# One block's forward and backward pass: weight-gradient products dealt out in pieces

## The chip, the cores and the metric

The kernel runs on one core of a Trainium2 chip. The metric is device time in microseconds of one execution, lower is better. The kernel before took 1703.19 us (median of three runs, 1692.96 to 1707.07). Profiles are of one execution each, with instructions per engine, waits and DMA transfers. TensorE (PE) multiplies matrices, VectorE (DVE) and ScalarE (ACT) do elementwise work, GpSimd (POOL) issues some DMAs and gathers, SyncE (SP) issues most DMAs.

## The reference

A transformer-like block with modulation (adaLN) is run forward, and then all its gradients are taken. x is 2048 tokens by 1024 features, the MLP is 1024 to 3584 to 1024, everything is bf16.

```python
def _A_ref(x, w_r, w_i):              # spectral mixer
    X = rfft2(x.astype(float32))
    return irfft2(X * (w_r + 1j * w_i), s=(S, D)).astype(bfloat16)

def _B_ref(x, w1, b1, w2, b2):        # MLP
    y = _layernorm(x)
    h = _gelu(einsum('bsd,df->bsf', y, w1) + b1)
    return einsum('bsf,fd->bsd', h, w2) + b2

mod = (_silu(c) @ w_mod).reshape(1, 6, 1, -1)
sa, ca, ga, sb, cb, gb = (mod[:, r] for r in range(6))
x = A_x
h = _layernorm(x) * (1 + ca) + sa
x = x + ga * _A_ref(h, A_w_r, A_w_i)
h = _layernorm(x) * (1 + cb) + sb
x = x + gb * _B_ref(h, B_w1, B_b1, B_w2, B_b2)
out, vjp = jax.vjp(f, A_x, A_w_r, A_w_i, B_w1, B_b1, B_w2, B_b2, c, w_mod)
return (out, *vjp(grad_out))
```

Outputs are out_0 (the block's result) and out_1 to out_9: gradients of x, of the spectral weights (out_2, out_3), of w1 (out_4), b1, w2 (out_6), b2, c (out_8) and w_mod (out_9).

## The kernel before, in words

Tokens are handled in four blocks of 512 (4 tiles of 128). The Fourier transforms are matrix products with cosine and sine matrices, with even and odd halves folded. The stages in code order, with the times they take in the profile:

- *Start and forward spectral mixer* (0 to some 305 us). `spectral_core` makes the forward product over tokens (`s_fwd`, matmuls "pu"), eight `pair` steps (matmuls "pcs" over features, then DVE work that multiplies with w_r and w_i and writes rows of R), the inverse over tokens (`s_inv`, matmuls "pv", four classes CE, SE, CO, SO of 32 matmuls), and four output steps (matmuls "po", then `consume`, a long DVE and ACT chain). The products "pp" (L610, gradient through w2) run beside it.
- *MLP* (389 to 864). `z_block(b, g0, g1)` makes groups g0 to g1 of the seven hidden groups of block b: 32 matmuls "pz", then gelu and its derivative on ACT and DVE; h goes to an SBUF slot (eleven in a ring) and to DRAM (d_hh), the gradient to DRAM (d_gz). `bo_pass(b, h)` makes half h of the output product: seven pieces of 16 matmuls "pbo", one per hidden group, into four PSUM banks; then eviction, the product with grad_out, its column sum "pa" on PE, and the store of out_0. The order is `z_block(b, 0, 4)`, `bo_pass(b-1, 1)`, `z_block(b, 4, 7)`, `bo_pass(b, 0)`.
- *Backward through w1 and layer norm* (864 to 1142): matmuls "pg", then DVE and ACT work per block, which ends in fbuf2, the input of the backward spectral pass.
- *Backward spectral pass and w2 gradient* (1078 to 1457). The second `spectral_core`, with `consume_bwd` as its output step; behind it in code order the w2 gradient: 28 chunks of 128 hidden rows, each one transposed load of d_hh and two products of 16 matmuls "gw2acc" with gB (grad_out times the gb row).
- *w1 gradient* (1457 to 1701): seven blocks of 512 hidden columns, each two transposed loads of d_gz (gzh) and eight products of 16 matmuls "gw1acc". Between them the gradient of w_mod: six rows r of 1024 values (d_gmod, fp32), broadcast to all partitions and cast; per row eight loads of w_mod, eight outer-product tiles stored to out_9 (gww) and eight reductions (wrw).

PSUM has tags "s" and "d" with two banks each and "f" with four; gw2acc, gw1acc, pbo, pp and pg use "f". SBUF tiles share buffers by tag: a tile of one tag must be free before the next one of that tag is written.

The order of the instructions in each engine's queue is fixed when the kernel is built: a planner takes the operations with code order as their priority and with estimated times, so that later code may be drawn forward where an engine would stand idle by the estimate. `tc.high_priority()` moves an operation ahead; `nc.any` leaves it to the planner whether ACT or DVE does it. Waits on the chip are by semaphore, and an engine does not pass the instruction at the head of its queue.

Of the kernel before, what the change touches and what calls it, by code (L numbers as in the profile page):

```python
# [10 lines left out]
FP32 = mybir.dt.float32  # L11
# [6 lines left out]
P = 128  # L18
# [12 lines left out]
NB = 4  # L31
# [4 lines left out]
def kernel(  # L36
# [74 lines left out]
    d_gmod = dram.tile([6 * D], FP32, name="d_gmod")  # L111
# [58 lines left out]
    def store_gmod(accs, r):  # L170
        for h in range(2):
            row = small.tile([1, KH], FP32, tag="gmrow", bufs=1)
            nc.vector.tensor_copy(out=row[:], in_=accs[h][0:1, :])
            nc.sync.dma_start(out=d_gmod[r * D + h * KH:r * D + (h + 1) * KH].rearrange("(o n) -> o n", o=1), in_=row[:])
# [234 lines left out]
    def spectral_core(fwd, fb, sms, em, css, pt, evac_u, evac_c, evac_v, consume, o4tag, pfs=None):  # L409
# [83 lines left out]

        for cl in (CE, SE, CO, SO):
            Us[cl] = s_fwd(cl, fb, sms[cl % 2][:, cl // 2], evac_u)
# [14 lines left out]
        for par in range(2):  # L510
            for m in range(4):
                pair(par * 4 + m, par, m)
        for cl in (CE, SE, CO, SO):
            s_inv(cl, smis[cl % 2])
        ct = reg.tile([P, 4, 4, D], BF16, name="ct", tag=o4tag)
        xts = [reg.tile([P, 4, D], BF16, name="xt", tag=tg)[:] for tg in ("sma", "smb")]
        for i in range(4):
            o4 = ct[:, 3 * (i % 2)]
            for cl in range(4):
                for hh_ in range(2):  # L520
                    po = ps_d("po")
                    for d2 in range(2):
                        dc = 2 * hh_ + d2
                        for h in range(2):
                            gi = 2 * dc + h + (4 if (dc >= 2 and cl >= 2) else 0)
                            nc.tensor.matmul(po[:, d2 * 256:(d2 + 1) * 256], lhsT=Vs[cl][:, 2 * dc + h, i * P:(i + 1) * P],  # L526
                                             rhs=gm[:, gi, :], start=(h == 0), stop=(h == 1))
                    with tc.high_priority():
                        nc.any.tensor_copy(out=o4[:, cl, hh_ * 512:(hh_ + 1) * 512], in_=po[:])
            consume(i, o4, ct[:, 1 + i % 2], xts[i % 2])  # L530

# [156 lines left out]
    def bo_pass(b, h):  # L688
# [4 lines left out]
        for g in range(7):  # L693
            wp = w2p[w2n[0] % 4]
            w2n[0] += 1
            nc.sync.dma_start(out=wp, in_=w2_v[:, g * 4:(g + 1) * 4, cs_])
            hh = hh_slots[(b * 7 + g) % 11]
            for i in range(4):
                for k in range(4):
                    nc.tensor.matmul(pbs[i][:], lhsT=hh[:, k, i * P:(i + 1) * P], rhs=wp[:, k, :],  # L700
                                     start=False, stop=(g == 6 and k == 3))
        bo, x1t, go = (otile[:, k] for k in range(3))
# [5 lines left out]
        tt(go, go, bo, ALU.mult)  # L708
        pa = ps_d("pa")
# [6 lines left out]
        tt(bo, bo, bcn(gb_row[:, cs_], 4), ALU.mult)  # L716
        tt(bo, bo, x1t, ALU.add)
        store_tok_half(out_0, bo, b, h)
# [9 lines left out]
    nc.sync.dma_start(out=d_gmod[5 * D:6 * D].rearrange("(o n) -> o n", o=1), in_=gacc)  # L728
# [81 lines left out]
    store_gmod(accS, 3)  # L810
    store_gmod(accC, 4)
# [21 lines left out]
    hh_o = [0, 1, 0, 1] + [2, 3, 0, 1] * 6  # L833
# [4 lines left out]
    def consume_bwd(i, o4, tmp, n1):  # L838
# [21 lines left out]
        if i == 3:  # L860
            store_gmod(accCA, 1)

    spectral_core(False, fbuf2, (smA2, smB2), em2, [css2[:, 0], css2[:, 1]],
                  new_pair_temps(["t0", "t1", "t2", "t3"]), act_copy, act_copy, act_copy, consume_bwd, "fr", pfs)


    gwo = reg.tile([P, 2, D], BF16, name="gwo", tag="ph")
# [5 lines left out]
    for fc in range(NFC):  # L873
        nc.sync.dma_start_transpose(out=hh_s[hh_o[fc]], in_=d_hh[fc * P:(fc + 1) * P, :])
        if fc >= NFC - 2:
            continue
        ob = gwo[:, fc % 2]
        for h in range(2):
            acc = ps_f("gw2acc")
            for t in range(NT):  # L880
                gw2_mm(acc, fc, h, t)
            with tc.high_priority():
                nc.scalar.copy(out=ob[:, h * KH:(h + 1) * KH], in_=acc[:])  # L883
        nc.gpsimd.dma_start(out=out_6[fc * P:(fc + 1) * P, :], in_=ob)
    last = [(fc, h, ps_f("gw2acc")) for fc in (NFC - 2, NFC - 1) for h in range(2)]
    for b in range(NB):
        for fc, h, acc in last:
            for t in range(4 * b, 4 * b + 4):
                gw2_mm(acc, fc, h, t)
    for fc, h, acc in last:  # L890
        with tc.high_priority():
            nc.scalar.copy(out=gwo[:, fc % 2, h * KH:(h + 1) * KH], in_=acc[:])
        if h == 1:
            nc.gpsimd.dma_start(out=out_6[fc * P:(fc + 1) * P, :], in_=gwo[:, fc % 2])

    n3ns = []
    for b in range(NB):
        n3n = reg.tile([P, 4, D], BF16, name=f"n3n{b}", tag=f"t{b}")
        nc.sync.dma_start(out=n3n[:], in_=chunk_rows(d_n3, b))
        n3ns.append(n3n)  # L900
    gzh = [reg.tile([P, 8, 512], BF16, name=f"gzh{k}", tag=PXT[2 + k]) for k in range(4)]
    gwo1 = reg.tile([P, 4, 512], BF16, name="gwo1", tag="ph")

    def gw1_load(fg):
        for k in range(2):
            ins = nc.sync.dma_start_transpose(out=gzh[2 * (fg % 2) + k][:], in_=d_gz[fg * 512:(fg + 1) * 512, k * 1024:(k + 1) * 1024])  # L906
        return ins

    def gw1_block(fg):
        gz2 = gzh[2 * (fg % 2):2 * (fg % 2) + 2]  # L910
        for cch in range(NDC):
            acc = ps_f("gw1acc")
            for t in range(NT):
                nc.tensor.matmul(acc[:], lhsT=n3ns[t // 4][:, t % 4, cch * P:(cch + 1) * P], rhs=gz2[t // 8][:, t % 8, :],  # L914
                                 start=(t == 0), stop=(t == NT - 1))
            ob = gwo1[:, (fg * NDC + cch) % 4]
            with tc.high_priority():
                nc.scalar.copy(out=ob, in_=acc[:])  # L918
            nc.gpsimd.dma_start(out=out_4[cch * P:(cch + 1) * P, fg * 512:(fg + 1) * 512], in_=ob)  # L919

    gw1_load(0)
    gw1_block(0)
# [3 lines left out]
    for b in range(NB):  # L926
# [7 lines left out]
    store_gmod(accGA, 2)  # L934
# [6 lines left out]
    nc.sync.dma_start(out=d_gmod[0:D].rearrange("(o n) -> o n", o=1), in_=sr[0:1, 0, 0, :])  # L941

    u_bfc = small.tile([P, NDC], BF16, tag="u_bfc", bufs=1)
    nc.vector.tensor_copy(out=u_bfc[:], in_=u_col[:])
    u_rt = small.tile([P, NDC], FP32, tag="u_rt", bufs=1)
    nc.vector.tensor_copy(out=u_rt[:], in_=u_bfc[:])
    gr = [reg.tile([P, 2, D], FP32, name=f"gr{k}", tag=f"uv{k}") for k in range(2)]
    wrw = reg.tile([P, 4, D], BF16, name="wrw", tag="uv2")
    gww = reg.tile([P, 4, D], BF16, name="gww", tag="uv3")
    nn = 0  # L950
    for ri, r in enumerate((5, 3, 4, 1, 2, 0)):
        with tc.issue_after(gw1_load(1 + ri).ins):
            grep_ = gr[ri % 2][:, 0, :]
            gbf = gr[ri % 2][:, 1, 0:KH].bitcast(BF16)
            nc.sync.dma_start(out=grep_, in_=d_gmod[r * D:(r + 1) * D].partition_broadcast(P))
            nc.vector.tensor_copy(out=gbf, in_=grep_)
            for jc in range(NDC):
                wr = wrw[:, nn % 4, :]
                gw = gww[:, nn % 4, :]
                nn += 1  # L960
                nc.sync.dma_start(out=wr, in_=w_mod[jc * P:(jc + 1) * P, r * D:(r + 1) * D])
                nc.vector.tensor_scalar(out=gw, in0=gbf, scalar1=u_rt[:, jc:jc + 1], scalar2=None, op0=ALU.mult)
                nc.gpsimd.dma_start(out=out_9[jc * P:(jc + 1) * P, r * D:(r + 1) * D], in_=gw)  # L963
                nc.vector.tensor_tensor_reduce(out=wr, in0=wr, in1=gbf, scale=1.0, scalar=0.0,
                                               op0=ALU.mult, op1=ALU.add, accum_out=gu[:, r, jc:jc + 1])
        gw1_block(1 + ri)
# [41 lines left out]
```

## Time and profile before

| | before |
|---|---|
| time, median of three runs | 1703.19 us |
| the profiled execution's own time | 1712.4 us |
| its span | 1710.6 us |
| PE busy | 1493.2 us (87%) |
| DVE busy | 1066.1 us (62%) |
| ACT busy | 742.0 us (43%) |
| POOL busy | 370.8 us (22%) |
| mean granted TensorE clock | 0.949 |

How to read it: the slices cut the span into 40 equal parts of 42.8 us and give each engine's busy share in tenths. A matmul's busy time overlaps with the next one's, so counts per stretch say more than busy time. A wait is written as engine, what it was about to do, and who ended the wait. A group of instructions is given with its count, busy time, mean length in ns and the idle time before it. In the DMA list stand the count, the size of one and the median time from issue to landing.

### The profile page before, as it was taken

To read this page: it belongs to the slowest core of one execution; us is meant where nothing else is said; L and a number is where in the kernel's file an instruction comes from. 1 tells how busy PE (TensorE), PEld (TensorE's weight loads), DVE (VectorE), ACT (ScalarE), POOL (GpSimd) and SP (SyncE) were. 2 spreads that over 40 slices of the span, in tenths; PEclk is the share of its full clock that TensorE was granted. 3 is DMA by queue.
4 is the path that set the end of the run, shared out by engine and by line. 5 is a ranking of instruction groups with operands and counts; after the bars stand their busy time and mean duration, and the time that the engine had idled before them with its cause. 6 is when DMAs were issued, how large, how long until landed. Compare 5 with 4: busy or idle time off the path is not lost. (4 is left out here: it accounts for less than half of the span.)

```text
span 1710.6 us, 18308 instructions
## 1 busy us (share of the span) xinstructions
PE 1493.2 (87%) x6692; PEld 684.6 (40%) x6826; DVE 1066.1 (62%) x1536; ACT 742.0 (43%) x1001; POOL 370.8 (22%) x421
## 2 busy tenths in 40 slices
PE   3689999998869998999789999879779879988787
PEld 2234545443324343444334444335334434433333
DVE  3586477785878776776304788845566969164341
ACT  2675556868557565565122333234234432211111
POOL 3340361110111222112110002403441211122222
PEclk9899999999989999999899999889999989999889
DMA  9962577898466756799952553554576598889993
GB/s 301 231 181 74 123 213 247 254 256 198 160 200 207 224 189 215 243 250 245 244 162 87 185 173 107 200 129 93 148 162 189 153 236 199 207 286 231 237 216 87
DMA packets 380288, 331.12 MB, mean 194 GB/s; under 512 B 230171, under 2 KB 321307, under 8 KB 380070
## 3 DMA queue, kind: packets, MB, share of 16 engines
q1 hardware_dynamic: 344310, 212.44, 50.4%
q0 software_dynamic: 33792, 114.36, 20.2%
q10 hardware_dynamic: 2096, 3.15, 0.6%
q8 instruction: 53, 0.87, 0.2%
q14 instruction: 37, 0.30, 0.1%
HBM read 168.34 MB, written 108.06 MB: 162 GB/s over the span
## 5 line engine op out<-in xcount | busy, mean ns | idle before, releaser
L914 PE MATMUL gw1acc<-gzh,n3n 128*128 128x512 bf16 x877 | 203.1, 391 | 28.1 <-ACT gwo L918 25.0
L610 PE MATMUL pp<-gBoT,wt 128*128 128x512 bf16 x874 | 203.8, 385 | 3.4 <-DVE phr L617 1.4
L778 PE MATMUL pg<-w1T,gzr 128*128 128x512 bf16 x878 | 196.6, 380 | 5.1 <-ACT otile L707 3.8
L914 PEld LDWEIGHTS <-n3n 128*128 128x128 bf16 x896 | 89.9, 100 | 141.0 <-issue 41.5
L664 PEld LDWEIGHTS <-w 128*128 128x128 bf16 x896 | 89.9, 100 | 115.2 <-issue 15.3
L610 PEld LDWEIGHTS <-wt 128*128 128x128 bf16 x896 | 89.3, 100 | 108.6 <-issue 9.5
L778 PEld LDWEIGHTS <-gzr 128*128 128x128 bf16 x896 | 87.7, 98 | 111.0 <-issue 6.0
L870 PE MATMUL gw2acc<-gB,hhsA 128*128 128x512 bf16 x500 | 119.6, 392 | 5.7 <-DVE gB L168 3.1
L918 ACT CAST gwo<-gw1acc 128x512 bf16<-128x512 f32 x56 | 32.0, 587 | 207.3 <-DMA out_dram<-gwo 116.0
L168 DVE TENSOR_TENSOR gt<-gt,gt 128x2048 bf16<-128x2048 bf16 x84 | 101.7, 1222 | 24.5 <-ACT gt L672 23.2
L664 PE MATMUL pz<-n3Ta,w 128*128 128x512 bf16 x437 | 102.5, 392 | 2.3 <-ACT gt L667 1.4
L870 PE MATMUL gw2acc<-gB,otl 128*128 128x512 bf16 x374 | 94.6, 402 | 9.7 <-DMA otl<-d_hh 9.2
L664 PE MATMUL pz<-n3Tb,w 128*128 128x512 bf16 x441 | 101.5, 388 | 0.6
L700 PEld LDWEIGHTS <-hhA 128*128 128x128 bf16 x608 | 59.6, 99 | 94.3 <-DVE hhA L168 16.2
L667 ACT ACTIVATE gt<-pz,b_col 128x512 bf16<-128x512 f32 x112 | 71.9, 684 | 56.6 <-PE pz L664 53.0
L883 ACT CAST gwo<-gw2acc 128x512 bf16<-128x512 f32 x52 | 30.1, 584 | 117.2 <-PE gw2acc L870 99.7
L489 PE MATMUL pv<-smi,R 128*128 128x512 bf16 x249 | 62.5, 397 | 20.4 <-DVE R L168 18.6
L870 PEld LDWEIGHTS <-hhsA 128*128 128x128 bf16 x512 | 51.8, 101 | 69.1 <-issue 13.3
L168 DVE TENSOR_TENSOR ct<-ct 128x2048 bf16<-128x2048 bf16 x64 | 75.6, 1217 | 3.9 <-ACT ct L370 3.8
L668 ACT ACTIVATE gt<-gt 128x2048 bf16<-128x2048 bf16 x28 | 53.5, 1911 | 43.6 <-DMA d_gz<-gt 43.3
L671 ACT ACTIVATE gt<-gt 128x2048 bf16<-128x2048 bf16 x28 | 53.5, 1911 | 42.5 <-DVE gt L168 42.5
L870 PEld LDWEIGHTS <-otl 128*128 128x128 bf16 x384 | 39.8, 104 | 56.9 <-DMA otl<-d_hh 9.7
(272 smaller groups left out, 2502.4 us busy)
## 6 DMA issues: line engine op xcount, KB each, us to landing
d_gz<-gt POOLq DMA_DIRECT2D x28, 512.0 KB, 6.3
gzr<-d_gz SPq DMA_DIRECT2D x28, 512.0 KB, 4.8
wrw<-in_w_mod_dram SPq DMA_DIRECT2D x48, 256.0 KB, 4.9
out_dram<-gww POOLq DMA_DIRECT2D x48, 256.0 KB, 4.8
wblk<-in_w_mod_dram SPq DMA_DIRECT2D x11, 1024.0 KB, 22.9
d_ph<-pho POOLq DMA_DIRECT2D x21, 512.0 KB, 5.3
d_hh<-hhA POOLq DMA_DIRECT2D x19, 512.0 KB, 5.1
w2sD<-in_B_w_dram SPq DMA_DIRECT2D x14, 512.0 KB, 6.7
```

The lines of the kernel that those rows point to most:

```text
L168: nc.vector.tensor_tensor(out=out, in0=a, in1=b, op=op)
L489: nc.tensor.matmul(pv[:], lhsT=R[:, cl * 4 + m, :, :].rearrange("p x w -> p (x w)")[:, base:base + 255:2], rhs=smi[:, cl // 2, m, :], star ...
L610: nc.tensor.matmul(pp[:], lhsT=wt[:, fg % 2, cch, k * P:(k + 1) * P], rhs=gBoT[j][:, cch, :], start=(cch == 0), stop=(cch == NDC - 1))
L664: nc.tensor.matmul(pz[:], lhsT=w1s[g][:, cch, k * P:(k + 1) * P], rhs=n3T[:, cch, :], start=(cch == 0), stop=(cch == NDC - 1))
L667: nc.scalar.activation(out=zb[:, k, :], in_=pz[:], func=ACT.Identity, bias=b1_col[:, fc:fc + 1], scale=1.0)
L668: nc.scalar.activation(out=av, in_=zb, func=ACT.Square)
L671: nc.scalar.activation(out=sg, in_=bv, func=ACT.Sigmoid, scale=2.0 * GK)
L700: nc.tensor.matmul(pbs[i][:], lhsT=hh[:, k, i * P:(i + 1) * P], rhs=wp[:, k, :], start=False, stop=(g == 6 and k == 3))
L778: nc.tensor.matmul(pgs[i][:], lhsT=gzt[g][:, k, i * P:(i + 1) * P], rhs=w1Ts[g][:, k, h * KH:(h + 1) * KH], start=(g == 0 and k == 0), sto ...
L870: nc.tensor.matmul(acc[:], lhsT=hh_s[hh_o[fc]][:, t, :], rhs=gBs[t // 4][:, t % 4, h * KH:(h + 1) * KH], start=(t == 0), stop=(t == NT - 1))
L914: nc.tensor.matmul(acc[:], lhsT=n3ns[t // 4][:, t % 4, cch * P:(cch + 1) * P], rhs=gz2[t // 8][:, t % 8, :], start=(t == 0), stop=(t == NT ...
L918: nc.scalar.copy(out=ob, in_=acc[:])
```

## The change

Four things are changed.

1. `bo_pass` becomes a generator that stops after each of its seven pieces; its column sum pa comes after a further stop. `z_block` groups and pieces are called in turn: two groups, two pieces, one group, two pieces and so on (`Z_AT`). The column sum of a half runs one or two pieces into the next half.
2. The w2 and w1 gradients become one generator, `pieces`, of 112 pieces of 16 matmuls (the last two chunks of w2 go by quarters). `spectral_core` calls `fill(n)`: 12 pieces before the token product, 4 after each pair, 6 after each consume step. In all 68 are asked for inside, then 3 in each of the four steps of the accGA sums, and the other 32 at the end. The first eight d_hh chunks use two slots (hh_o), later ones four. Evictions are left to either ACT or DVE, and the w1 results have eight slots for four.
3. The first three w_mod rows (5, 3, 4) are issued with blocks 0, 1 and 2 of the w1 gradient, the other three (1, 2, 0) with blocks 3, 4 and 5; the loads of d_gz are issued one block ahead. The rows are kept in bf16, so the broadcast has half the bytes and no cast follows. A row is stored to d_gmod by one DMA.
4. In both spectral passes `s_inv` of CE and SE comes ahead of the last two pairs. The products of grad_out with the gb row have high priority.

```diff
-    d_gmod = dram.tile([6 * D], FP32, name="d_gmod")
+    d_gmod = dram.tile([6 * D], BF16, name="d_gmod")
...
+        fill(12)
         for cl in (CE, SE, CO, SO):
             Us[cl] = s_fwd(cl, fb, sms[cl % 2][:, cl // 2], evac_u)
...
         for par in range(2):
             for m in range(4):
+                if par == 1 and m == 2:
+                    s_inv(CE, smis[0])
+                    s_inv(SE, smis[0])
                 pair(par * 4 + m, par, m)
-        for cl in (CE, SE, CO, SO):
-            s_inv(cl, smis[cl % 2])
+                fill(4)
+        s_inv(CO, smis[1])
+        s_inv(SO, smis[1])
...
             consume(i, o4, ct[:, 1 + i % 2], xts[i % 2])
+            fill(6)
...
+    Z_AT = {0: (0, 2), 2: (2, 3), 4: (3, 4), 8: (4, 5), 10: (5, 6), 12: (6, 7)}
     z_block(0, 0, 7)
-    bo_pass(0, 0)
-    for b in range(1, NB):
-        z_block(b, 0, 4)
-        bo_pass(b - 1, 1)
-        z_block(b, 4, 7)
-        bo_pass(b, 0)
-    bo_pass(NB - 1, 1)
+    for b in range(NB):
+        steps = bo_both(b)
+        for k in range(14):
+            if b + 1 < NB and k in Z_AT:
+                z_block(b + 1, *Z_AT[k])
+            next(steps)
+            if bo_late and k % 7 in (1, 2):
+                for late in bo_late:
+                    next(late, None)
+                bo_late.clear()
...
-        tt(gb_t[:], gb_t[:], bcn(gb_row, 4), ALU.mult)
+        with tc.high_priority():
+            tt(gb_t[:], gb_t[:], bcn(gb_row, 4), ALU.mult)
...
-    hh_o = [0, 1, 0, 1] + [2, 3, 0, 1] * 6
+    hh_o = [0, 1] * 4 + [2, 3, 0, 1] * 5
...
+    def pieces():
+        for fc in range(NFC):
+            nc.sync.dma_start_transpose(out=hh_s[hh_o[fc]], in_=d_hh[fc * P:(fc + 1) * P, :])
+            for h in range(2 if fc < NFC - 2 else 0):
+                acc = ps_f("gw2acc")
+                for t in range(NT):
+                    gw2_mm(acc, fc, h, t)
+                gw2_out(acc, fc, h)
+                yield
...
+        gw1_load(0)
+        for fg in range(F // 512):
+            if fg < 6:
+                ins = gw1_load(fg + 1)
+                if fg < 3:
+                    gmod_row(fg, ins)
+                else:
+                    w1g[fg] = ins
...
+            for cch in range(NDC):
+                acc = ps_f("gw1acc")
...
+                with tc.high_priority():
+                    nc.any.tensor_copy(out=ob, in_=acc[:])
+                nc.gpsimd.dma_start(out=out_4[cch * P:(cch + 1) * P, fg * 512:(fg + 1) * 512], in_=ob)
+                yield
...
+        fill(3)
         for q in range(4):
             colsum(accGA, gxa[:, q, :], b == 0 and q == 0, b == 3 and q == 3)
...
+    fill(56 + 24 - done[0])
+    for ri in range(3, 6):
+        fill(1)
+        gmod_row(ri, w1g[ri])
+        fill(7)
+    fill(8)
```

More of the change, by code (lines that the diff above doesn't have):

```diff
@@ L925, with fill @@
+    todo = pieces()
+    done = [0]
+    def fill(n):
+        for _ in range(n):
+            next(todo)
+        done[0] += n
+    spectral_core(False, fbuf2, (smA2, smB2), em2, [css2[:, 0], css2[:, 1]],
+                  new_pair_temps(["t0", "t1", "t2", "t3"]), act_copy, act_copy, act_copy, consume_bwd, "fr", pfs, fill)
     accGA = [ps_s("accGA0"), ps_s("accGA1")]
@@ L940 @@
     unfold_d(sr[0:1, 0], sr[0:1, 1])
[L941 to L966, printed above, removed]
+    store_gmod([sr[0:1, 0, 0, 0:KH], sr[0:1, 0, 0, KH:D]], 0)
+    assert done[0] <= 56 + 24
+    fill(56 + 24 - done[0])
[4 more added lines that the diff above has]
+    fill(8)
     t9 = small.tile([P, 5, NDC], FP32, tag="t9", bufs=1)
```

130 lines of the change are left out of this document (75 added, 55 removed).

## The prediction

> **What bounds the kernel now.** I read the page first, with its 40 slices.
>
> ```profile
> span 1710.6 us, 18308 instructions
> ...
> PE   3689999998869998999789999879779879988787
> ...
> PEclk9899999999989999999899999889999989999889
> DMA  9962577898466756799952553554576598889993
> ```
>
> TensorE (PE) is at 8 or 9 tenths in most slices, and where it is short of 9 the granted clock is mostly under full too. Busy time hides part of that, so I counted instead. These are stretches that I cut by hand (columns: stretch, length, then busy us and count for PE, weight loads, DVE, ACT, POOL, then granted clock, DMA share, GB/s). Every matmul has its weight load, and the load records are the more complete, so I count loads.
>
> ```profile
> 598.50:641.25 42.75, 42.54 (x194) 18.99 (x197) 30.60 (x47) 26.34 (x28) 8.82 (x9) 1.00 0.56 189
> 389.00:510.00 121.00, 91.81 (x383) 39.13 (x390) 84.13 (x135) 79.51 (x77) 13.55 (x18) 0.90 0.64 180
> 510.00:797.00 287.00, 272.42 (x1200) 120.67 (x1224) 206.89 (x300) 169.79 (x157) 57.62 (x61) 0.97 0.75 225
> 797.00:864.00 67.00, 55.06 (x237) 23.70 (x240) 26.06 (x44) 13.17 (x11) 8.35 (x9) 0.90 1.08 259
> 1078.00:1142.00 64.00, 47.21 (x188) 19.84 (x191) 49.23 (x67) 16.89 (x23) 13.00 (x10) 0.84 0.56 155
> 1182.00:1300.00 118.00, 95.41 (x401) 44.16 (x407) 69.78 (x89) 38.82 (x65) 50.65 (x34) 0.93 0.67 168
> 1300.00:1457.60 157.60, 139.46 (x662) 67.45 (x674) 130.37 (x175) 60.78 (x78) 23.87 (x28) 0.95 0.72 185
> 1457.60:1510.00 52.40, 46.12 (x203) 20.53 (x206) 9.93 (x8) 7.51 (x13) 7.97 (x13) 0.97 0.79 211
> 1510.00:1701.00 191.00, 165.02 (x711) 72.79 (x724) 81.37 (x154) 25.56 (x45) 50.34 (x93) 0.93 0.95 218
> 1701.00:1710.60 9.60, 0.14 (x1) 0.00 (x0) 0.00 (x0) 0.59 (x1) 0.54 (x1) 0.75 0.04 15
> ```
>
> The first row is a dense stretch: 42.75 us / 197 = 0.217 us per matmul. Length minus count x 0.217 is what a stretch loses. MLP: 121 - 84.6 = 36.4, 287 - 265.6 = 21.4 and 67 - 52.1 = 14.9. Backward: 64 - 41.4 = 22.6 up to the forward DFT, and 118 - 88.3 = 29.7 in the pairs. In 1300 to 1457.6 (the consume steps) some 120 matmuls are half as wide,
>
> ```profile
> 1300.00:1457.60 157.60, 18.45 (x120) 10.12 (x15) 9.70 (x17) 0.95 0.72 185
> ```
>
> (the po matmuls, all on record), so 157.6 - 614 x 0.217 = 24.4. The w1 gradient loses 52.4 - 44.7 = 7.7 and 191 - 157.1 = 33.9. What the change can win lies in these terms. PE's own waits say what they are made of:
>
> ```profile
> PE gw1acc L914 <- ACT gwo L918: 25.0, 6, 10.1
> PE pv L489 <- DVE R L168: 18.6, 5, 5.1
> PE pbo L700 <- DVE hhA L168: 14.7, 3, 10.9
> PE po L526 <- ACT ct L529: 13.7, 4, 7.7
> PE pa L711 <- DVE otile L168: 11.6, 4, 4.9
> ```
>
> PE's timeline shows how such a wait looks, and that gw2 products already fill single gaps between spectral steps:
>
> ```profile
> 1199.77 0.42 PE L870 MATMUL gw2acc<-gB,hhsA 128*128 128x512 bf16 x1
> ...
> 1210.90 1.04 PE L489 MATMUL pv<-smi,R 128*128 128x512 bf16 x2 [4.88 <-DVE R L168]
> ```
>
> ```profile
> 1130.83 9.96 PE L870 MATMUL gw2acc<-gB,otl 128*128 128x512 bf16 x33 [9.21 <-DMA otl<-d_hh]
> ```
>
> At 1206 PE stood for 4.88 us before two pv matmuls: their place in PE's queue was fixed too early for the row of R that DVE had to finish. After the 9.21 us wait, 33 matmuls took 9.96 us and not 7.2: 2.8 us more at a lower clock.
>
> **Part by part.** *(a) MLP output product in pieces.* The columnsum pa moves from directly behind a pass to one or two pieces into the next. Its passes, and so nearly all of the 11.6 us of waits, lie in 510 to 797. That stretch loses 21.4; without these waits 10 remain, and I give 6 of those to the clock that they cost. So up to 17 goes. What is late next is the hand-over between the two halves of one block, where the next pass needs the four PSUM banks at once. An eviction of 128x512 takes:
>
> ```profile
> L918 ACT CAST gwo<-gw1acc 128x512 bf16<-128x512 f32 x56 | 32.0, 587 | 207.3 <-DMA out_dram<-gwo 116.0
> ```
>
> Four of 0.587 are 2.3 us, at four boundaries 0 to 9; I take 4, since a z group stands behind to be drawn forward. Is gelu work fast enough to feed an even mix? One z group and two pieces are 64 matmuls, 13.9 us of PE.
>
> ```profile
> 510.00:797.00 287.00, 140.78 (x613) 51.55 (x79) 0.97 0.75 225
> ```
>
> That row has the pz matmuls alone: 613/32 = 19.2 groups, so DVE spends 206.9/19.2 = 10.8 us per group and ACT 8.8. PE stays the bound. The pieces take their w2 loads along on SP, evenly spread and not in runs, which costs nothing while the DMA share is 0.75. The start (36.4: DVE hh waits, gelu must run ahead first) and the end (14.9: w2 loads at DMA share 1.08) keep their cause. Net 13; bounds -15 (an even mix that keeps running into hh or the banks, about 0.75 us on each of 20 groups) to +30.
>
> *(b) Before the forward DFT.* The first eight hh chunks now use two slots and need no otl, so the 9.2 us and its 2.8 go. Against it:
>
> ```profile
> hhsA<-d_hh SPq DMA_TRANSPOSE x16, 7.2
> ```
>
> A chunk lands in 7.2 us and its 32 matmuls take 6.9, so with two slots each of six later chunks may come up to 1 us late; I take 4. The gB products get priority on DVE; this can move at most their own time ahead of the layer-norm chain, and two of the four already stood ahead of it:
>
> ```profile
> 1076.02 4.49 DVE L168 TENSOR_TENSOR gB<-gB,rows 128x4096 bf16<-128x4096 bf16 x2
> ```
>
> Zero for that, cover being the gw2 products. Net 8, bounds -5 to 18.
>
> *(c) Pairs.* Each pair is now 16 pcs and four pieces of 16: 80 matmuls, 17.4 us. DVE's 69.8 us over at most eight pairs, plus what ran before 1182, is near 10 us a pair. So DVE is done with R before PE comes to pv: CE and SE are asked for two pairs after their last row, CO and SO behind four pieces. The 18.6 us go, and of the other 11.1 I give 6 to the clock. New: a piece whose chunk is late, or an eviction that now can land on DVE: 5. Net 19; bounds 5 to 27. In the forward pass only the place of CE and SE changes; PE is at 9 tenths in slices 5 to 9, so 0 (+-3).
>
> *(d) Consume steps.* Here PE waits for consumers (13.7 us on ct), and DVE is busy 130.4 of 157.6. Three modulation rows come in:
>
> ```profile
> L964 DVE CUSTOM_DVE_ANT_0 wrw<-wrw,gr 128x1024 bf16<-128x1024 bf16 x48 | 57.9, 1213 | 3.3 <-DMA wrw<-in_w_mod_dram 3.3
> ...
> L962 DVE TENSOR_SCALAR gww<-gr,u_rt 128x1024 bf16<-128x1024 bf16 x48 | 23.7, 500 | 4.1 <-DMA out_dram<-gww 4.0
> ```
>
> 24 x (1.213 + 0.500) = 41 us of DVE work, and gz transposes on SP's queue:
>
> ```profile
> 1460.19 34.95 SPq L906 DMA_TRANSPOSE gzh<-d_gz  x4
> ```
>
> 8.7 us each; six to eight of them are 52 to 70 us of SP time in front of the loads of x and gx1 and the stores of out_1. POOL gets 24 more stores. The pieces behind each consume step (6 x 3.47 = 20.8 us of PE) cover part of it. Net 0; bounds -30 to +12.
>
> *(e) w1 gradient.* PE waits 25.0 us for an eviction, and the eviction mostly (116.0 us of ACT's idle time in the row under (a)) for the store of its slot. The stretch ran at DMA share 0.95. Sizes:
>
> ```profile
> wrw<-in_w_mod_dram SPq DMA_DIRECT2D x48, 256.0 KB, 4.9
> out_dram<-gww POOLq DMA_DIRECT2D x48, 256.0 KB, 4.8
> ...
> out_dram<-gwo POOLq DMA_DIRECT2D x56, 128.0 KB, 5.1
> ...
> gr<-d_gmod SPq DMA_DIRECT2D x6, 512.0 KB
> ```
>
> A block with a row moves 4096 KB for the row, 512 for the broadcast, 1024 of results and two gz tiles of 1024: 7.9 MB, six of them 47 MB less the gz that came early; 191 us x 218 GB/s is 41.6. Afterwards four blocks are left behind the spectral part, three with a row (the broadcast halved, 7.6 MB) and one without (3.1): 25.9 MB, 119 us at 218 GB/s, against 4 x 128 x 0.217 = 111 of PE. So 8 lost there, the 8 around the accGA sums stay, and 5 for start-up: 21 instead of 41.6. Eight result slots for four help, and either engine may evict. Net 20; bounds 5 to 33. The bf16 rows also drop six casts and one of two small stores per row on SP, which no product waits for. The 9.6 us behind the last product stay.
>
> Sum: 13 + 8 + 19 + 0 + 20 = 60. The profiled execution took 1712.4 us (span 1710.6), so 1652 by that; it lies 9 above the median of 1703.2, against which I forecast 1643.
>
> The Trainium skill's page "TensorE: Matmul & The Clock Gate" (Part 1, the HAM clock gate) says that PE falls to half clock after an idle window of about 3.4 us and needs a busy window to recover. By that rule a wait under 3.4 us would cost nothing more, a longer one at most 1.7 us, and (a) and (c) together would be some 3 us smaller. The 2.8 us after the 9.21 us wait is more than that; I keep the measured side.
>
> **Rivals.** *R1, the gain is only moved.* The transfers of three rows and of three gz blocks land in the consume steps, beside 185 GB/s that is there already; PE's accCA and po then wait longer. (d) becomes -25 and (a) to (e) leave 35 at best; with (e) at 5, 20: 1683. For it: gz transposes of 8.7 us on SP. Against: share 0.72 there. The Trainium skill, page "DMA: Bandwidth & Descriptors", section "Issuing engines are not separate DMA queues", speaks for this case: all queues run on the same 16 engines, so dealing work onto other moments helps only where those are idle. No run here shows it yet.
>
> *R2, nothing moves.* The order was already interleaved (the single gw2 matmul at 1199.77), and the planner's timing errors come back in other places: 1703.
>
> *R3, slower.* The rows' DVE work stands in front of the consume chain: 130.4 + 41 = 171 us of DVE alone, plus what SP's 52 to 70 us of transposes hold back. PE's queue contains po and accCA at fixed places, so it is held with them. It decides once the consume steps run more than the 60 us won elsewhere over: at 157.6 + 85, for 1728. Against: the rows come behind the chain in code order.
>
> *R4, all listed waits go:* a 20, b 18, c 27, d 10, e 33: 108, so 1595.
>
> **Numbers.** Forecast 0.50 (1615 to 1670), R1 0.20, R2 0.13, R3 0.12, R4 0.05. From no change, 1% (17 us) can be told apart. Faster: 0.50 + 0.05 + two thirds of R1 = 0.68; same: R2 and the rest of R1, 0.20; slower 0.12. The range runs from 1600 (all of R4 but its end) to 1705, taking in R2 and leaving out R3 and little else.
>
> **What would show it.** (a) pa has no wait and 510 to 797 is shorter by 10 to 20. (b) no wait for otl before the DFT. (c) pv waits for R nearly gone, gw2 in runs of 16 to 64 between pairs. (d) consume steps about as long as now; if accCA, po or accGA waits grow past 40 us, R1 or R3. (e) the waits of gw1acc on its eviction under 10 us, the end free of modulation rows. I am wrong if PE's lost time per stretch falls by less than 20 us in sum, or if one new wait on DVE or SP takes it back.

## The result, and the profile after

The changed kernel took 1652.99 us (median of four executions, 1647.19 to 1656.89), against 1705.13 us for the kernel before on the same chip (1692.96 to 1713.14). The ratio is 0.970, with a 95% interval of 0.963 to 0.976. The profiled execution took 1654.47 us with a span of 1652.7 us, 57.9 less than the span of before.

The first part of the page of the changed kernel, with its slices:

```profile
span 1652.7 us, 18418 instructions
...
PE   3788999999598987999979999979999997889796
```

PE's slices 28 to 33 (1116 to 1364 us) are now all nines: that is the token product, the pairs and the first consume steps. 7, 8, 8 follow in the later consume steps, a 7 (slice 38) at the accGA sums, and the last slice is a 6. The same stretches cut by hand (columns as in the prediction):

```profile
510.00:797.00 287.00, 270.50 (x1210) 118.60 (x1209) 223.23 (x333) 172.90 (x159) 57.90 (x61) 0.96 0.76 228
...
1076.40:1132.70 56.30, 47.81 (x209) 20.78 (x208) 49.73 (x70) 14.96 (x18) 10.68 (x10) 0.91 0.56 163
...
1160.50:1326.30 165.80, 165.80 (x770) 80.39 (x769) 91.18 (x118) 50.88 (x83) 45.85 (x46) 1.00 0.67 178
1326.30:1482.00 155.70, 130.15 (x625) 63.16 (x624) 128.73 (x180) 54.59 (x72) 36.57 (x45) 0.93 0.79 211
1482.00:1544.50 62.50, 51.32 (x228) 22.49 (x226) 48.92 (x74) 12.14 (x17) 18.19 (x28) 0.91 0.93 270
1544.50:1638.30 93.80, 93.61 (x433) 42.10 (x431) 40.55 (x79) 15.11 (x26) 27.89 (x50) 1.00 1.06 224
1638.30:1652.70 14.40, 0.00 (x0) 0.00 (x0) 0.00 (x0) 0.59 (x1) 0.54 (x1) 0.67 0.31 53
```

With the prediction's measure, length less count of loads x 0.217 us (the 128 half-wide po matmuls of the consume steps count half), PE's lost time is, in us:

| stage | before | after |
|---|---|---|
| MLP and pg products together, as a length | 389 to 1078: 689.0 | 387 to 1076.4: 689.4 |
| up to the forward DFT | 22.6 | 56.3 - 45.1 = 11.2 |
| pairs | 29.7 | 0 |
| consume steps | 24.4 | 155.7 - 121.5 = 34.2 |
| accGA sums | 7.7 | 62.5 - 49.0 = 13.5 |
| w1 gradient behind them | 33.9 | 93.8 - 93.5 = 0.3 |
| behind the last product | 9.6 | 14.4 |

The six lower rows fall by 54 us in sum, which is nearly all of the 57.9. (The MLP row shows no gain in these two executions. What that part is worth is measured below.) Three rows went to nothing or to half, and three became worse: PE stands less before the DFT, not at all in the pairs and the late w1 blocks, and longer in the consume steps, at the accGA sums and at the end. PE's waits (engine, what it was about to do, who ended the wait: total us, times, longest) show the same:

```profile
PE pbo L698 <- ACT otile L715: 15.6, 4, 8.8
...
PE accCA L178 <- DVE ct L168: 13.7, 4, 7.7
PE accGA L178 <- DVE gxa L168: 11.2, 2, 10.3
PE pz L670 <- ACT gt L673: 9.9, 5, 5.4
...
PE po L531 <- ACT ct L534: 5.9, 3, 3.7
PE pbo L706 <- DVE hhA L168: 5.8, 2, 4.3
...
PE pbo L706 <- DMA w2sA<-in_B_w_dram: 2.1, 1, 2.1
...
PE pa L724 <- DVE otile L168: 0.9, 1, 0.9
```

The waits for R (18.6), for otl (9.2) and for the gw1acc evictions of line 918 (25.0) are gone, and pa's 11.6 is 0.9. New at the top is a wait of the first pbo matmuls (line 698, the bias row) for four PSUM banks. The waits of accCA and accGA, the column sums in and behind the consume steps, were small before:

```profile
PE accGA L178 <- DVE gxa L168: 4.2, 1, 4.2
...
PE accCA L178 <- DVE ct L168: 1.7, 2, 1.1
```

PE's timeline of the pairs shows runs where single matmuls stood before:

```profile
1160.51 1.89 PE L427 MATMUL pcs<-empf,U 128*128 128x256 bf16 x8
...
1164.36 13.59 PE L899 MATMUL gw2acc<-gB,hhsA 128*128 128x512 bf16 x62
...
1264.11 13.98 PE L489 MATMUL pv<-smi,R 128*128 128x512 bf16 x64
```

Each pair is 16 pcs and 64 gw2 matmuls, 17.3 us, and the 64 pv matmuls of CE and SE start without a wait.

### The profile page after: what moved, and what is told of

It is laid out like the page before. It is cut to its first block, busy times and chain, and to the rows that moved or that the text cites. A ratio compares the mean times of both kernels' runs of the same rounds, so it can differ in the third digit from the quotient of the medians.

```text
span 1652.7 us, 18418 instructions
## 1 busy us (share of the span) xinstructions
PE 1483.8 (90%) x6826; PEld 679.9 (41%) x6826; DVE 1074.8 (65%) x1546; ACT 734.7 (44%) x989; POOL 360.3 (22%) x421
## 4 chain that ended last, share of the span: by engine, by line
PE 33%; DMA 10%; DVE 9%; issue 7%; ACT 3%; POOL 2%; SPq 0%; POOLq 0%; ACTq 0%; DVEq 0%
PE gw2acc L899 10%; PE pg L805 5%; PE pbo L706 5%; PE pz L670 3%; PE gw1acc L972 2%; DVE got L767 2%; PE pu L403 2%; PE pcs L427 2%; PE pv L489 2%; DMA d_gz<-gt 2%; DVE ct L168 2%; DMA xt<-d_gx 1%; DVE gn3a L772 1%; DMA wrw<-in_w_mod_dram 1%; DMA gB<-in_grad_out_dram,xu 1%
## 5 line engine op out<-in xcount | busy, mean ns | idle before, releaser
L972 PE MATMUL gw1acc<-gzh,n3n 128*128 128x512 bf16 x896 | 197.9, 382 | 6.2 <-ACT gwo L904 6.0
L899 PE MATMUL gw2acc<-gB,hhsA 128*128 128x512 bf16 x576 | 130.2, 383 | 3.3 <-DVE gB L168 3.3
L673 ACT ACTIVATE gt<-pz,b_col 128x512 bf16<-128x512 f32 x112 | 71.5, 684 | 35.7 <-PE pz L670 33.9
L899 PEld LDWEIGHTS <-hhsA 128*128 128x128 bf16 x576 | 57.3, 100 | 71.4 <-issue 5.2
L674 ACT ACTIVATE gt<-gt 128x2048 bf16<-128x2048 bf16 x28 | 53.3, 1908 | 64.3 <-DMA d_gz<-gt 64.0
L899 PE MATMUL gw2acc<-gB,otl 128*128 128x512 bf16 x320 | 71.5, 380 | 0.0
L545 DVE CAST cs01b<-pcs 128x512 bf16<-128x512 f32 x16 | 11.1, 693 | 82.5 <-PE pcs L427 82.5
L928 DVE CUSTOM_DVE_ANT_0 wrw<-wrw,gr 128x1024 bf16<-128x1024 bf16 x48 | 58.0, 1215 | 5.0 <-DMA wrw<-in_w_mod_dram 4.9
```

What stands on the lines that cost most here:

```text
L673: nc.scalar.activation(out=zb[:, k, :], in_=pz[:], func=ACT.Identity, bias=b1_col[:, fc:fc + 1], scale=1.0)
L674: nc.scalar.activation(out=av, in_=zb, func=ACT.Square)
L899: nc.tensor.matmul(acc[:], lhsT=hh_s[hh_o[fc]][:, t, :], rhs=gBs[t // 4][:, t % 4, h * KH:(h + 1) * KH], start=(t == 0), stop=(t == NT - 1))
```

## The experiments

The theory to be tested was the prediction's: each edit is worth its term, and the dealing of the products is worth (c). The rivals were R2 for single edits (the planner does it anyway) and R1 (what is won in one place is paid in another). Ratios are to the kernel before, measured on the same chip within the same series; the repeat of the changed kernel, with no edit, gives the scale.

> The changed kernel once more, unchanged, beside the three next ones, so that they are compared on the same chip. Expected as on record: 0.963 to 0.976 of before.

Measured: 1653.35 us, 0.9685 (0.9632 to 0.9737). A few us between two kernels can't be told apart by these intervals of about 0.005 to each side; there the profiles' stages and waits decide.

### The MLP part alone, and everything but it

First, the kernel before with only the MLP part of the change (edit 1):

```diff
-    z_block(0, 0, 7)
-    bo_pass(0, 0)
-    for b in range(1, NB):
...
+    for b in range(NB):
+        steps = bo_both(b)
...
```

> The kernel before with the MLP part of the change alone (pieces of the output product between the gelu groups, the column sum moved into the next half). My theory after reading the profile of the changed kernel: the waits for pa go (11.6 us), but the hand-over of the four PSUM banks waits behind a Square on ACT instead (15.6 us there), so the time stays, 1703 to 1713. The rival, which is term (a) of the prediction: 13 us less, 1690.

Measured: 1701.43 us, 0.9937 (0.9909 to 0.9965): 11 us faster, 6 to 16. My theory of no gain fell; term (a)'s 13 us lies inside that interval. Then the changed kernel with the old order of the MLP:

```diff
-    for b in range(NB):
-        steps = bo_both(b)
...
+    bo_pass(0, 0)
+    for b in range(1, NB):
+        z_block(b, 0, 4)
+        bo_pass(b - 1, 1)
+        z_block(b, 4, 7)
+        bo_pass(b, 0)
+    bo_pass(NB - 1, 1)
```

> The changed kernel with the old order of the MLP. My theory: no loss, 1643 to 1653, the whole gain being in the backward part. The rival: 13 us more than the changed kernel, 1666.

Measured: 1667.03 us, 0.9732 (0.9675 to 0.9788), against 0.9685 and 0.9697 for the changed kernel: 6 to 8 us slower, which the interval alone doesn't settle. The time is near the rival's 1666, and not the 1643 to 1653 that I expected. PE's waits of m2 in these stages say what the order changes:

```profile
PE pbo L706 <- DVE hhA L168: 14.5, 3, 9.6
...
PE pbo L706 <- DMA w2sA<-in_B_w_dram: 11.9, 2, 11.1
PE pa L717 <- DVE otile L168: 9.1, 3, 4.7
...
PE pg L784 <- ACT otile L713: 4.0, 1, 4.0
```

Without the new order the waits for h (hhA, 14.5), for pa (9.1), for the w2 loads of the last passes (11.9) and for the banks at the first pg products (4.0) are there; with it they are 5.8, 0.9, 2.1 and none. Against that stand the 15.6 us at the banks and 9.9 instead of 1.8 us for gelu's banks (pz). Added up over the waits of pz, pbo, pa and the first pg, PE waits 57.6 us in the changed kernel and 64.3 in m2; in the other pair it is 50.2 in m1 and 57.3 in the kernel before. Net about -7, in both pairs of kernels. So (a) is worth some 7 to 11 us and was forecast at 13.

The table's MLP row shows nothing of this, because another wait came in: pbo for hhB, 5.3 us before and 14.1 in the changed kernel. It is 14.0 in m2 with the old order and 6.3 in m1 with the new one, so the order of the MLP alone does not make it; which of the other edits does was not tried.

### The wait for four banks

Why does the hand-over between two halves cost 15.6 us where I took 4? ACT's and PE's timeline of the changed kernel around the longest wait:

```profile
643.57 1.91 ACT L674 ACTIVATE gt<-gt 128x2048 bf16<-128x2048 bf16 x1 [5.92 <-DMA d_gz<-gt]
645.39 2.03 ACT L715 CAST otile<-pbo 128x512 bf16<-128x512 f32 x4
646.00 1.55 PE L698 MATMUL pbo<-b_row,ones_bf 1*128 1x512 bf16 x3 [8.82 <-ACT otile L715]
```

PE waits 8.82 us for an eviction that takes half a microsecond. The evictions stand in ACT's queue behind a gelu instruction (line 674), and that waited 5.92 us for its gt buffer, which the store to d_gz still read. So this bank wait is a DMA wait, passed on by ACT's queue. The second longest, at the last hand-over, has another cause:

```profile
834.64 1.07 ACT L715 CAST otile<-pbo 128x512 bf16<-128x512 f32 x2 [7.28 <-DMA out_dram<-otile,xu]
835.28 0.58 PE L698 MATMUL pbo<-b_row,ones_bf 1*128 1x512 bf16 x1 [6.33 <-ACT otile L715]
```

Here nothing stands ahead of the evictions; they wait themselves, for the one output tile, which the store of the half before still reads. The two waits make 15.2 of the 15.6 us. Two ways around the first one were tried. The evictions on DVE:

```diff
-                nc.scalar.copy(out=bo[:, i, :], in_=pbs[i][:])
+                nc.vector.tensor_copy(out=bo[:, i, :], in_=pbs[i][:])
```

> The changed kernel with the evictions of the MLP output product on VectorE and not on ScalarE. If the hand-over waits because those evictions stand behind gelu's Square in ACT's queue, which itself waits for the store of d_gz, the 15.6 us of waits for banks go and the kernel takes some 1638. The rival: DVE's queue holds them up just as well, or the late store of the output tile does, and it stays at 1653.

Measured: 1668.36 us, 0.9756 (0.969 to 0.9821). My expectation of 1638 fell: the wait changed its engine and grew.

```profile
PE pbo L698 <- DVE otile L715: 24.4, 4, 11.3
```

```profile
844.31 0.69 DVE L715 CAST otile<-pbo 128x512 bf16<-128x512 f32 x1 [12.76 <-DMA out_dram<-otile,xu]
```

The wait behind the gelu work is 6.17 us for 8.82: DVE, with 10.8 us a group before the busier of the two in the MLP, has work of its own in front of the evictions. What grew is the last hand-over, 17.1 us for 6.33, where the evictions waited 12.76 and 5.67 us for the store of the output tile, as the rival had it. The other way is a z group exactly at the hand-over, so that PE has something to do there:

```diff
-    Z_AT = {0: (0, 2), 2: (2, 3), 4: (3, 4), 8: (4, 5), 10: (5, 6), 12: (6, 7)}
+    Z_AT = {0: (0, 1), 2: (1, 2), 4: (2, 3), 7: (3, 4), 9: (4, 5), 11: (5, 6), 13: (6, 7)}
```

> The changed kernel with the gelu groups dealt so that one stands right ahead of the first piece of each half (groups at steps 0, 2, 4, 7, 9, 11, 13 and not two at 0 and none between 4 and 8). If the hand-over of the four banks costs PE what the waits say (15.6 us of waits for evictions, most of it in two places), a group of 6.9 us there covers about half: 6 to 12 us less than the changed kernel. The rival: PE then waits for the gelu chain at that place instead, no change.

Measured: 1658.92 us, 0.9698 (0.9636 to 0.976), no gain, and the bank wait rose to 23.3 us: 13.3 of it at the last hand-over, where an eviction waited 14.02 us for the store of the output tile, and 8.4 at the place of the 8.82. So neither run took away what it was meant to, and both lengthened the wait for the output tile; why the store came later there, the runs don't show. A second output tile, which would test that half of the wait, was not tried.

### The dealing inside the spectral pass

The changed kernel without the pieces that are dealt out, so that all of w2 and w1 stand behind the spectral pass in code order, as before, with the rest of the change kept:

```diff
-                  ..., act_copy, act_copy, act_copy, consume_bwd, "fr", pfs, fill)
+                  ..., act_copy, act_copy, act_copy, consume_bwd, "fr", pfs)
...
-        fill(3)
         for q in range(4):
             colsum(accGA, ...)
```

> The changed kernel with all 112 weight-gradient pieces behind the spectral pass and the accGA sums in code order, none dealt out; s_inv, slots, bf16 rows, evictions and MLP as changed. My theory: the planner draws pieces forward only into gaps that it foresees, so pv waits for R and the consume steps have less beside them: 1680 to 1710. The rival R2 of the prediction: the planner does as well without the dealing, 1650 to 1660.

Measured: 1662.01 us, 0.9703 (0.9644 to 0.9762): as fast as the changed kernel within the interval, which leaves room for some us: all four executions of d1 (1656.87 to 1664.23) lie at the slowest of the eight of the changed kernel and its repeat (1656.89) or above it. My own expectation (1680 to 1710) fell, and R2's 1650 to 1660 was missed by 2 us. The windows of d1, from the first gw2 product on (up to the pairs, pairs and pv, consume steps, w1 gradient, end):

```profile
1078.50:1162.00 83.50, 73.47 (x322) 32.40 (x328) 51.87 (x72) 32.25 (x48) 10.51 (x10) 0.94 0.53 140
1162.00:1288.00 126.00, 107.62 (x467) 53.23 (x475) 80.70 (x106) 45.98 (x77) 54.38 (x36) 0.92 0.66 169
1288.00:1447.80 159.80, 140.87 (x662) 67.56 (x673) 135.10 (x182) 59.47 (x75) 25.35 (x29) 0.96 0.70 188
1447.80:1648.50 200.70, 197.02 (x892) 89.33 (x909) 84.92 (x154) 32.82 (x56) 58.68 (x106) 0.99 0.91 252
1648.50:1658.00 9.50, 0.85 (x4) 0.20 (x2) 0.00 (x0) 0.59 (x1) 0.54 (x1) 0.69 0.04 14
```

and the waits of d1's spectral pass:

```profile
PE pv L489 <- DVE R L168: 14.4, 4, 8.8
...
PE accCA L178 <- DVE ct L168: 5.4, 2, 2.8
...
PE accGA L178 <- DVE gxa L168: 2.7, 1, 2.7
```

By the same measure d1 loses 12.3, 22.9, 27.6, 3.4 and 9.5 us, 75.7 in sum; the changed kernel loses 73.6 (the table's six rows). Without dealing the wait for R is back at 14.4 and the pairs lose 22.9. With it they lose nothing, but the consume steps lose 34.2 for 27.6, the accGA sums and the w1 gradient 13.8 for 3.4, the end 14.4 for 9.5: 21.9 of the 22.9 are paid behind. Among the waits, accCA is 13.7 for 5.4 and accGA 11.2 for 2.7. That is R1's mechanism. And the w1 stage with the accGA sums loses 3.4 in d1 where it lost 41.6 before: so the large gain of the change is there, and it comes without the dealing.

### What freed the w1 gradient

Only eight result slots, in the kernel before (the edit also gives them a buffer of their own, "wt", where they had shared "ph" with the w2 results):

```diff
-    gwo1 = reg.tile([P, 4, 512], BF16, name="gwo1", tag="ph")
+    gwo1 = reg.tile([P, 8, 512], BF16, name="gwo1", tag="wt")
...
-            ob = gwo1[:, (fg * NDC + cch) % 4]
+            ob = gwo1[:, (fg * NDC + cch) % 8]
```

> The kernel before, with eight result slots for the w1 gradient and not four, nothing else. In the undealt version the w1 stretch runs without waits, 43 us shorter than before; if that is because an eviction need no longer wait for the store of its slot, this kernel alone gains 25 to 40 us: 1665 to 1680. The rival: the bound is the transfers of six rows of w_mod beside the transposed loads (218 GB/s in that stretch, as the prediction's term (e) had it), the stores land late all the same, and it gains under 10: 1695 to 1705.

Measured: 1688.43 us, 0.9879 (0.9824 to 0.9934): some 20 us, between the two expectations. The converse, four slots in the changed kernel, still in "wt":

```diff
-        gwo1 = reg.tile([P, 8, 512], BF16, name="gwo1", tag="wt")
+        gwo1 = reg.tile([P, 4, 512], BF16, name="gwo1", tag="wt")
...
-                ob = gwo1[:, (fg * NDC + cch) % 8]
+                ob = gwo1[:, (fg * NDC + cch) % 4]
```

> The changed kernel with four result slots and not eight. If the slots carry the gain, the waits of gw1acc on its eviction come back, some 20 to 30 us: 1673 to 1683. The rival, the spreading of the rows carries it: 1653 to 1660.

Measured: 1667.19 us, 0.9752 (0.9696 to 0.9808): 14 us slower than the changed kernel's repeat in that series, with no overlap between their executions, and two thirds of the eviction wait of 25.0 us is back:

```profile
PE gw1acc L972 <- ACT gwo L976: 17.1, 4, 12.8
```

So the slots are worth 14 to 20 us, the larger figure together with the buffer. In g1 PE's next wait in the w1 gradient is for the transposed loads:

```profile
PE gw1acc L914 <- DMA gzh<-d_gz: 19.2, 6, 8.3
```

My theory for these 19.2 us was the place of the rows in code order; so g1 with each row one block earlier:

```diff
-        gw1_block(1 + ri)
+        if ri:
+            gw1_block(ri)
+    gw1_block(6)
```

> The kernel before with eight result slots for the w1 gradient, and in code order each row of the w_mod gradient one block earlier (the first two rows ahead of block 1, the last block free of rows). Theory: what is left after eight slots alone (19.2 us of PE's waits for the transposed gz loads) comes from the rows' loads and stores standing in front of the gz loads of the next blocks, above all of the last one. Then these waits fall under 8 us, and the ratio to the kernel before is 0.972 to 0.981, 10 to 20 us better than eight slots alone (0.9879). Rival: it takes the bf16 rows or the dealing to bring the loads early, and the ratio stays at 0.985 to 0.990.

Measured: 1693.04 us, 0.9908 (0.987 to 0.9947), no faster than g1. The theory fell as put: the wait for gz fell to 10.8 us, but g4 gained nothing. SP's timeline of g4 shows that the edit did not do what I meant it to: the first row still starts behind the loads of gxa, at 1501 (the last of these is issued at 1493).

```profile
1501.12 3.84 SPq L955 DMA_DIRECT2D gr<-d_gmod  x2
```

In the kernel before the rows' tiles (gr, wrw, gww) share buffers with gxa and ata, so no row can start before the accGA sums are done, wherever it stands in code. The change gives them other buffers ("sb", "px1" and otl), a part of the diff to which the prediction gave no price. In d1 the first row starts at 1463. What a late start leads to is seen in SP's queue of g1, where one row and the two gz loads of a block take turns:

```profile
1573.66 0.57 SPq L955 DMA_DIRECT2D gr<-d_gmod  x1
1574.32 11.64 SPq L961 DMA_DIRECT2D wrw<-in_w_mod_dram  x8
1586.06 25.65 SPq L906 DMA_TRANSPOSE gzh<-d_gz  x2
1611.76 0.57 SPq L955 DMA_DIRECT2D gr<-d_gmod  x1
```

and in d1:

```profile
1547.99 11.21 SPq L925 DMA_DIRECT2D wrw<-in_w_mod_dram  x8
1564.77 10.47 SPq L913 DMA_TRANSPOSE gzh<-d_gz  x2
1575.30 0.58 SPq L922 DMA_DIRECT2D gr<-d_gmod  x1
```

In g1 a round takes 38.1 us on SP, where PE needs 128 x 0.217 = 27.8 us for a block: SP is behind, and a pair of transposed loads that runs directly after the row's loads takes 25.65 us. In d1 SP has time to spare (5.6 us between the rows' last load and the transposes), and the same pair takes 10.47. A round then costs what PE costs. The longer pair alone does not hold PE up, though. The changed kernel has it too, in its last blocks:

```profile
1557.25 21.19 SPq L913 DMA_TRANSPOSE gzh<-d_gz  x2
```

That round takes 33.4 us, the next 30.8, and yet PE loses 0.3 us in that stretch. Only three rows are left there and the loads are issued one block ahead; that this is the reason is likely, but it was not tried. That the early start of the rows is what keeps d1 on the good side is read from these timelines; it was not tried by itself, and the halved broadcast (256 KB for 512) and the choice of engine for the evictions changed with it.

The last piece is how early the rows have to be. The changed kernel with no row beside the consume steps and two with each of blocks 3, 4 and 5:

```diff
-                if fg < 3:
-                    gmod_row(fg, ins)
-                else:
-                    w1g[fg] = ins
+                w1g[fg] = ins
...
-        gmod_row(ri, w1g[ri])
+        gmod_row(2 * ri - 6, w1g[ri])
+        gmod_row(2 * ri - 5, w1g[ri])
```

> The changed kernel with all six rows of the w_mod gradient in the last blocks, two each with blocks 3, 4 and 5 of the w1 gradient; none is issued beside the consume steps. Theory (the rows load both ends): PE's waits in the consume steps and the accGA sums (accCA 13.7 and accGA 11.2 us with the early rows) fall to 5 each or less, so 10 to 15 us are won there; the last four blocks then move 6 x 4.6 + 4 x 3.1 = 40 MB, at 252 GB/s 159 us against 111 us of products, so 40 to 48 us are lost there. Sum 25 to 38 us slower than the changed kernel, ratio 0.983 to 0.992. Rival (the early rows only move the load, the late blocks have room): within 8 us of it, ratio 0.964 to 0.973.

Measured: 1653.2 us, 0.9666 (0.9611 to 0.9721): as the rival had it, no slower. The theory's 25 to 38 us of loss did not come. PE's waits of r1 and its last two windows:

```profile
PE gw1acc L969 <- DMA gzh<-d_gz: 14.1, 1, 14.1
PE accCA L178 <- DVE ct L168: 6.0, 4, 3.4
...
PE accGA L178 <- DVE row L173: 0.4, 1, 0.4
```

```profile
1499.80:1626.50 126.70, 112.07 (x503) 50.30 (x511) 78.09 (x150) 19.16 (x33) 38.33 (x71) 0.95 1.04 278
1626.50:1648.40 21.90, 0.03 (x1) 0.00 (x0) 2.25 (x8) 0.58 (x1) 4.79 (x9) 0.61 0.74 73
```

The first half of my theory was right: without the rows accCA's wait falls from 13.7 to 6.0 us and accGA's from 11.2 to 0.4, and PE's last product starts at 1626, 12 us earlier than in the changed kernel. The loss at the end was oversized: 126.7 - 511 x 0.217 = 15.8 us, and a tail of 21.9 instead of 14.4. By the two windows some 37 MB moved there, most of it at 278 GB/s; I had reckoned with 40 MB at 252. It comes out even. So the early rows cost the consume steps and the accGA sums about what they save behind.

### The slots of hh

The changed kernel with the old slot order of the hh chunks:

```diff
-    hh_o = [0, 1] * 4 + [2, 3, 0, 1] * 5
+    hh_o = [0, 1, 0, 1] + [2, 3, 0, 1] * 6
```

> The changed kernel with the old slot order of the transposed hh chunks: chunks 4 and later may use the two slots that share a buffer with otl, which comes free late. Theory (step (b) of the prediction): the wait of some 9 us for otl ahead of the forward DFT comes back with its 2.8 us at a lower clock, 8 to 12 us slower than the changed kernel, ratio 0.973 to 0.976. Rival: now that products are dealt out, the planner finds other work for that stretch, or the time comes back in the consume steps, where PE waits anyway; ratio 0.967 to 0.971.

Measured: 1665.29 us, 0.9717 (0.9652 to 0.9782), between the two expectations, so the time doesn't settle it. PE's timeline of h1 does:

```profile
1130.23 15.31 PE L899 MATMUL gw2acc<-gB,otl 128*128 128x512 bf16 x62 [7.63 <-DMA otl<-d_hh]
```

The wait for otl is back with 7.6 us, and the matmuls behind it start slowly: 64 by their weight loads, in 15.4 us up to the next product, where 64 x 0.217 = 13.9; 1.5 more, 9.1 us in all. The way from the first gw2 product to the first pcs of the backward pass is 1172.7 - 1078.5 = 94.2 us in h1 and 1160.5 - 1076.4 = 84.1 in the changed kernel. By the ratios only 3 to 6 us of these 10 are left in the total.

### The end

Behind the changed kernel's last product, in ACT's timeline:

```profile
1644.20 0.59 ACT L976 CAST gwo<-gw1acc 128x512 bf16<-128x512 f32 x1 [8.73 <-DMA out_dram<-gwo]
```

The last eviction waits 8.73 us for its slot, whose store went out on POOL behind the last stores of the w_mod rows. So the stores of the last block on SP:

```diff
-                nc.gpsimd.dma_start(out=out_4[...], in_=ob)
+                (nc.sync if fg == 6 else nc.gpsimd).dma_start(out=out_4[...], in_=ob)
```

> The changed kernel with the stores of the last w1 block issued by SP and not by POOL. Theory: the 14.4 us behind the last product (9.6 before) come from these stores standing behind the last stores of the w_mod rows in POOL's queue; on SP, which has nothing left to load, the last store goes out at once. The tail falls to 8 to 10 us, and the ratio to the kernel before falls by 0.003 to 0.005 against the changed kernel (0.9685), to 0.964 to 0.966. Rival: the stores wait for the DMA engines, which are full then, and not for their queue: tail 13 to 15 us, ratio 0.968 to 0.971.

Measured: 1646.92 us, 0.9623 (0.9569 to 0.9677), as the theory had it and a little less, and the fastest of all kernels here. The window of t1 behind its last product:

```profile
1641.40:1649.50 8.10, 0.10 (x1) 0.00 (x0) 0.00 (x0) 0.58 (x1) 0.00 (x0) 0.70 0.61 98
```

The tail is 8.1 us for 14.4, and for 12.7 in the changed kernel's repeat. The intervals of t1 and of the changed kernel overlap, so the 5 to 6 us rest on the profiles.

## Why the prediction was right, and where its steps were not

The forecast sum was 60 us between profiled executions, and 57.9 were measured; 1643 was forecast and 1653 measured, 52 us between the medians. That the sum is so close is in part luck. By the table the terms came out as 0 for (a)'s 13, 11 for (b)'s 8, 30 for (c)'s 19, -10 for (d)'s 0, 28 for (e)'s 20 and -5 at the end for 0: errors of up to 13 us, of both signs. Most of the mechanisms were right, and these steps were not:

- *(a), 13 us.* Worth 7 to 11 by itself. The pa waits went as put (11.6 to 0.9), but the mark was wrong: 510 to 797 holds 1209 loads for 1224 and is no shorter. The failed term is the hand-over of the banks, taken as 4 us from the length of four evictions; it is 15.6, because I priced the evictions and neither ACT's queue in front of them nor the output tile that they write. What pays for it are waits that I had declared untouched: hhA (14.7 to 5.8), the late w2 loads (10.9 to 2.1) and the banks at the first pg products (3.8 to none). In the changed kernel the new hhB wait takes the rest.
- *(b), 8 us.* The loss before the DFT fell from 22.6 to 11.2; undone, it costs about 10 in that stretch. Right, somewhat undersized: the two slots did not make the chunks late.
- *(c), 19 us.* Locally right and more: no wait for R, and the pairs lose nothing (29.7 before). But d1 without the dealing is within the interval as fast. The step that failed is to count a closed gap in the pairs as gained: of the 22.9 us that the dealing takes out of the pairs, 21.9 come back behind them.
- *(d), 0 us.* Mis-sized: the consume steps lose 10 more, the accGA sums 6 more. R1's mechanism, inside the stated bounds (-30 to +12). The waits of accCA, po and accGA are 13.7 + 5.9 + 1.5 (a po wait for DVE's ct) + 11.2 = 32.3, under the 40 that I had set as the mark of R1. r1 shows that the rows' work is the cause of most: without it accCA and accGA fall by 18.5.
- *(e), 20 us.* Undersized: the w1 gradient with the accGA sums lost 41.6 and loses 13.8, and 3.4 in d1. The failed step is the ceiling of 218 GB/s, taken from a stage that was itself waiting: d1's w1 stage runs at 252 and r1's last blocks at 278. With 252 the 25.9 MB would take 103 us, less than the 111 us of PE, and the forecast 8 us of loss would have been none. Of the gain, 14 to 20 us are the eight slots, measured from both sides.
- *The tail* was to stay at 9.6 and became 14.4. I had priced who waits for the rows' stores and not what stands behind them in POOL's queue.

R2 was wrong as a whole and nearly right for the one edit that the change is named after. R3's point of decision, consume steps 85 us longer, was far off. Of the rows' 41 us of DVE work only some 18 lie in the consume steps, and some 12 us of the chain's own work moved behind them. Over the consume steps and the accGA sums together DVE is busy 177.7 us for 140.3, and the two are 218.2 us long for 210.0: most of the added work went into gaps.

What stays open: which of early rows, halved broadcast and free choice of the evicting engine takes the rest of (e) beside the slots; whether the place of CE and SE is worth anything by itself; what makes the hhB wait; what a second output tile would win; and whether late rows together with the last stores on SP would add their gains (r1's tail of 21.9 us suggests it). None of these was tried.

## What to carry to other kernels

A wait that is seen at PE can have its cause further back: before pricing an eviction by its own length, read what is ahead of it in ACT's, DVE's or POOL's queue, which of these instructions waits for a store, and whether a store still reads the tile that the eviction writes. Filling PE's gaps inside a dependent chain can move the loss to the chain's end, as 21.9 of 22.9 us did here, so ask what is late next, and look for the stage that is held by slots or by a shared buffer. A transfer rate read from a stage that waits is no ceiling.

## What the runs showed of the hardware that was not expected

- The two transposed loads of one gz block (2 MB) held SP for 10.47 us in d1 and for 25.65 us in g1, where they follow directly on a row's loads. The changed kernel has both prices, 10.13 us at 1438 and 21.19 us directly behind a row's loads at 1557. In g1 the queue had fallen behind; it paid 21.72, 25.65 and 22.05 us in three rounds running and stayed behind.
- 278 GB/s over 126.7 us with transposed loads, row loads and stores together (r1), where 218 GB/s at a DMA share of 0.95 had looked like the limit. The share alone did not tell the two apart (1.04 and 0.95).
- The slow start after a long wait has no fixed length. PE's weight loads stand 0.43 us apart at first and then 0.21: for 3.3 us after the 7.63 us wait in h1, which cost 1.5 us, and for 5.1 us after the 9.21 us wait before, which cost 2.4 (34 products by their loads in 9.8 us; the prediction's 2.8 counts 33). The Trainium skill's page "TensorE: Matmul & The Clock Gate" (Part 1, the HAM clock gate) has PE at half clock until at least one busy window of about 3.4 us has passed, from which the prediction's estimate was 1.7 us; h1 comes near that, the trace of before is above it, and "at most" was the prediction's word and not the page's.
